# Output projection over three and a half row chunks, with one head group spread into spare columns and half-row pairs

## The chip, the core and the metric

The kernel runs on one core of a Trainium2 chip. The metric is the device time of one launch in microseconds (us). Five engines work side by side, each through its own queue of instructions: TensorE (PE in the profile) multiplies matrices into the eight PSUM banks, VectorE (DVE), ScalarE (ACT) and GpSimd (POOL) do the elementwise work, and SyncE (SP) issues most of the DMAs.

## The reference

What is computed, cut to its parts (B = 1, S = 2048, D = 448, 16 heads of 28, four segments of 512, F = 1792, all in bf16):

```python
g = sigmoid((x * gate_w).sum(-1))                      # one gate per row of x
# a: attention with a memory, over N = 4 segments of L = 512
q, k, v = heads(x @ wq), heads(x @ wk), heads(x @ wv)
for s in range(4):
    p = softmax(qs @ ks.T * 28**-0.5 + causal_mask)
    a_dot = p @ vs
    a_mem = (phi(qs) @ M) / (phi(qs) @ z + 1e-6)       # phi(t) = t + 1 if t > 0 else exp(t)
    o = sigmoid(beta) * a_mem + (1 - sigmoid(beta)) * a_dot
    M += phi(ks).T @ vs ; z += phi(ks).sum(rows)
a = concat(o) @ wo
# b: a token-mixing MLP over the rows
b = (gelu(layernorm(x).T @ w1 + b1) @ w2 + b2).T
out = g * a + (1 - g) * b
```

## The kernel before

The program is written as a list of operations with their reads and writes (`op(...)`), and the order in which each engine runs them is written out in the dictionary `ORDER`, one text per engine. A word names an operation; `@4` gives the PSUM bank (or buffer) that it takes, and `u0-3*3` stands for three operations in a row. `plan` walks through these texts, gives out the banks and adds a wait wherever an operation reads or overwrites another's result. Each engine's queue is strictly in order.

The names that matter here:

- `lok`, `loq`, `lot` with `prk`, `prq`, `prx`, `prt`: the projections. The contraction over D = 448 rows is cut into three chunks of 128 rows and one of 64. Two outputs share one 128-row operation for their 64-row chunks: `lo...` runs two products of 64 rows, one on the upper and one on the lower half of the array, into two PSUM banks, and then each output's `pr...` adds its three full chunks. In `pair`, the `lo` comes first.
- `sc`, `exp`, `mask`, `pv`: scores of up to four heads side by side on four strips of 32 rows, their exponential on ScalarE into a probability buffer, the causal mask on GpSimd, and the product with the values. There is one set of four banks (0 to 3) for the scores, so that a score waits for the exponential before it. The other four banks (4 to 7) are shared by all the other products.
- Unit `u` = 4 * segment + head group. After `pv{u}`, VectorE transposes (`ta`), takes reciprocals (`rec`), scales both parts (`oa`, `om`); the sum (`o`) runs on GpSimd or VectorE into `ob[:, u % 2]`, and VectorE transposes it again (`ot`) into `oT`, which holds the queries' place in memory. In the first segment there is no memory part, and `oa` writes `ob` itself.
- `wo0` to `wo15`: the output projection of 128 rows each. A head has 28 rows but takes a strip of 32, so four head groups of four heads take four chunks of 128 rows in `oT`, with 16 idle rows in each. `wo_sb` holds the weights in the same layout, its spare rows zeroed once by a memset on VectorE (`wo0` there, `R_wo`), and filled by seven DMAs (`ldwo`). Each tile is four products of 128 rows by 448 columns. `ag` then applies the gate in ScalarE or VectorE.
- `u{ft}-{k}` (first MLP matrix, 14 x 16 products) and `y{T}-{ft}` (second, 16 x 14 products), `fin{T}` (VectorE, joins both parts) and `out{T}` (SP, store). Their weights stream through a ring of three slots (`ldw1`, `ldw2`), each loaded in four pieces.
- `gq`, `gk`: DMAs that gather the last head group of queries and keys from spare columns of the other three. `tk`: DMA transposes of the keys. `dtx`: those of x.

TensorE instructions come in layouts: full (128 rows by 128 columns), column-split (four of 128 by 32, used in stretches that also hold a `pv` or `mst`), pairs of 64 rows (`lo`), strips of 32 rows (`sc`), and 32 by 32 (`mem`).

Of the kernel before, what the change touches and what calls it, by code (L numbers as in the profile page):

```python
# [5 lines left out]
ACT = mybir.ActivationFunctionType  # L6
# [38 lines left out]

# [29 lines left out]
class Sched:  # L75
# [13 lines left out]
    def op(self, eng, fn, reads=(), writes=(), name=None, dma=False, out=False, cost=100.0, prio=0.0, mode="f",  # L89
           nbytes=0, rel=0.0, port=False, take=None, use=(), alt=None, space=None,  # L90
           hold=HOLD):
# [42 lines left out]
        for r in reads:  # L134
            if r.last_write is not None:
                need(r.last_write)
            if r.psum and eng != "PE":
                for rd in r.reads:
                    if rd.eng != "PE" and (rd.eng != o.eng or o.eng is None):
                        need(rd)  # L140
        for r in writes:
            w = r.last_write
# [8 lines left out]
        for r in writes:  # L151
            r.last_write = o
            r.reads = []
        self.ops.append(o)
        return o

    def plan(self, order):
# [17 lines left out]

        def ready(o, banks):
            users = [held.get((g.pool, int(b))) for g, b in zip(o.take, banks)]
            return all(d.idx in done for d in o.deps + o.order) and all(g is None or g.left == 0 for g in users)

        while any(queue.values()):  # L180
            n = len(line)
            for e in ENGINES:
                while queue[e] and ready(*queue[e][0]):
                    o, banks = queue[e].pop(0)
                    assert len(banks) == len(o.take)
                    for g, b in zip(o.take, banks):
# [102 lines left out]
btr@7 lok0_0 lok0_2 prk0_0 prx0_3 prk0_2 prk0_1 lok1_2@45 loq1_0@67 prk1_2 prq1_0 prx1_3 prq1_1 loq1_2@46 loq0_0  # L289
loq0_2 prq0_2 prq1_2 prq0_1 prq0_2h prq1_2h prq0_0 lot4@45 lot6@67 prt7 prt6 sc0_0 prt4 prt5 lok1_0@67 prk1_0 prk1_1  # L290
sc0_1 lok2_0@45 prk2_0 prk2_1 lok2_2@67 prx2_3 prk2_2 sc0_2 u0-0@4*3 u1-0@5*5 u0-3*3 u3-0@6 u1-5 u3-1 sc0_3 u0-6
u2-0@7*3 u3-2 u0-7 u2-3 u1-6*2 u2-4 u1-8*3 sc0_4 u0-8*7 u1-11*2 u0-15 u1-13*3 u2-5*3 sc1_0 u2-8*2 u3-3*5 u2-10*5
u3-8*2 sc1_1 u3-10 u5-0@4*3 u4-0@5 u2-15 u4-1 u3-11*3 u4-2 u3-14*2 u4-3 sc1_2 u4-4*3 u5-3 u4-7*3 pv1@7 u4-10*3
u5-4*4 u4-13*3 u6-0@6*3 sc1_3 u6-3 u5-8*2 pv0@7 u6-4 u5-10*5 sc1_4 u7-0@5*4 u6-5*4 u5-15 u6-9 mst0@7 sc2_0 u6-10*3
u7-4*2 u6-13*3 u8-0@4*2 u7-6*2 u8-2*3 u7-8 sc2_1 u7-9*2 pv2@6 u8-5 u7-11*3 u8-6 u7-14*2 sc2_2 loq2_0@67 prq2_0
u8-7*5 prq2_1 u8-12*4 mem1 loq2_2@57 prq2_2 prq2_2h u9-0@6*10 u10-0@5*2 u9-10*2 u11-0@7 sc2_3 u9-12*4 pv3@4 u11-1*7
sc2_4 u10-2*5 u11-8*2 pv4@4 u11-10 u12-0@6 sc3_0 u11-11*3 u10-7*2 u11-14*2 u10-9*2 u13-0@4*5 sc3_1 u10-11*3 u12-1
u10-14 pv5@7 u10-15 u13-5*4 u12-2*3 sc3_2 lot8@57 u12-5 prt9 u12-6 u13-9*4 sc3_3 u12-7*3 u13-13*2 u12-10*2 u13-15
u12-12*4 prt8 sc3_4 wo0#1@7 lok3_0@45 prk3_1 prk3_0 pv6@7 sc4_0 lot10@65 prt11 mst1@4 prt10 wo1@7 sc4_1 loq3_0@45
pv7@6 prq3_1 prq3_0 lok3_2@67 sc4_2 prk3_2 prx3_3 wo3@5 wo2@6 mem2 y1-0@4*6 y0-0@6*8 y1-6*3 sc4_3 loq3_2@57 prq3_2  # L300
prq3_2h y1-9*2 y0-8 y1-11*3 sc4_4 y0-9*5 y3-0@7 pv8@4 y2-0@5*2 sc5_0 y3-1 y2-2*2 y3-2*2 y2-4 y3-4*4 sc5_1 y2-5*4
wo5@4 y3-8*2 sc5_2 pv9@6 y3-10*3 wo4@4 y3-13 sc5_3 y2-9*3 y5-0@6 y2-12*2 wo6@7 sc5_4 y5-1*4 wo7@4 pv10@5 sc6_0
y5-5*8 pv11@4 sc6_1 mst2@5 y5-13 y6-0@7*7 sc6_2 lot12@45 prt12 y6-7*2 prt13 y6-9*2 mem3 lot14@64 prt14 prt15 y6-11*3
y4-0@6*3 sc6_3 y4-3*11 sc6_4 wo9@4 y7-0@5*2 wo8@6 sc7_0 pv12@7 y7-2*2 wo11@4 y7-4*2 sc7_1 y9-0@7*2 pv13@4 y7-6*4
y8-0@6 sc7_2 y8-1 y7-10*4 y8-2*2 y9-2*2 y8-4 y9-4 sc7_3 y9-5*3 wo10@4 pv14@5 y8-5 sc7_4 y8-6*3 y9-8 y11-0@5 y8-9*3
y9-9*3 y8-12*2 y11-1*7 pv15@4 y10-0@6 y11-8*5 y9-12*2 y10-1*5 y11-13 y10-6*8 wo15@4 wo13@5 wo14@6 y14-0@7*4
y15-0@4*3 y14-4 y15-3*2 y13-0@5 y14-5 y15-5 y13-1*2 y14-6 y13-3*2 y14-7*5 wo12@6 y13-5*4 y15-6 y13-9 y12-0@6*2
y13-10 y14-12*2 y12-2*3 y13-11*2 y12-5 y13-13 y12-6*8 y15-7*7 y15-0#1@5 y15-1#1 y15-2#1 y15-3#1 y15-4#1 y15-5#1
y15-6#1 y15-7#1 y15-8#1 y15-9#1 y15-10#1 y15-11#1 y15-12#1 y15-13#1""",
    "ACT": """  # L310
ldwv0 ldgw ldwv1 ldwv2 ldwvb ldwkb ldb1 ldb2 cpv2 cpv0 gt0 gt2 cpv1 gt3 gt1 ek0_0 cpk0_1 cpk0_3 cpk1_2 cpq1_0 cpq0_3
cpk1_3 ek0_1 cpq1_3 cpq1_2 cpq0_2 cpq1_1 cpq1_2#1 cpq0_2#1 cpq0_0 eq1_2 cpv7 cpv6 gt7 tb gt6 exp0_0@2 cpv5 gt4 gt5
cpk1_1 exp0_1@3 cpk2_1 cpk2_0 cpk2_3 cpk2_2 exp0_2@4 cpq2_3 ek0_2 exp0_3@0 eq1_1 eq1_0 exp0_4@1 gsq0 gsq1 gvh0
exp1_0@5 ek1_0 gth0 gth1 exp1_1@6 gsq2 eq1_3 gsq3 ek0_3 gvh3 gth2 exp1_2@0 gsq4 gth3 exp1_3@1 ek1_2 gth4 exp1_4@2
gsq5 ek1_1 exp2_0@3 gsq6 gth5 gvh6 exp2_1@4 gth6 gsq7 ek1_3 exp2_2@5 gth7 ek2_0 cpq2_0 gsq8 cpq2_2 eq2_1 cpq2_2#1
eq2_2 eq2_0 gvh8 exp2_3@6 gsq9 ek2_1 exp2_4@0 gth9 gth8 exp3_0@1 gsq11 gvh11 exp3_1@2 gsq10 gvh10 gth11 exp3_2@3
gth10 exp3_3@4 gsq13 gt9 gsq12 cpv8 gt8 exp3_4@0 cpk3_1 gth12 eq2_3 exp4_0@5 gt11 cpv10 gt10 ag1 exp4_1@6 gth13
cpq3_1 exp4_2@1 cpq3_0 ag2 eq3_0 cpk3_3 ag3 ek2_3 eq3_1 ek2_2 exp4_3@2 exp4_4@7 exp5_0@0 eq3_2 exp5_1@3 exp5_2@4
exp5_3@5 exp5_4@6 ag7 exp6_0@1 ag6 exp6_1@2 eq3_3 exp6_2@7 cpv12 gt12 cpv14 gt14 cpv15 gt15 cpv13 gt13 exp6_3@0
exp6_4@3 exp7_0@4 ag8 exp7_1@5 exp7_2@6 exp7_3@1 exp7_4@2 ag10 ag15 ag13""",  # L320
# [39 lines left out]
def build_kernel(nc, X, WQ, WK, WV, WO, BETA, W1, B1, W2, B2, GW, OUT):  # L360
# [796 lines left out]
    for u in range(16):  # L1157
# [5 lines left out]
        if u >= 4:  # L1163
            wo_tile(u - 4)
# [60 lines left out]
```

## Time and profile before

| | |
|---|---|
| time, median of 3 runs | 171.65 us (171.44 to 171.79) |
| the profiled execution's own time | 171.96 us |
| its span, first to last instruction | 170.2 us |
| TensorE busy | 166.1 us (98%), 2319 products |
| VectorE busy | 140.1 us (82%) |
| ScalarE busy | 130.7 us (77%) |
| GpSimd busy | 58.8 us (35%) |
| granted TensorE clock | 1.00 |
| moved by DMA | 25.16 MB, mean 148 GB/s |

The span is what the profile's times refer to; the launch takes 1.76 us beside it. Busy time is the union of an engine's instructions. In rows of groups and of the timeline stand the engine, the line of the kernel, the operation, output and input, and the count; a row of the timeline begins with its start and its length in us. Products overlap each other in the array, so that the length of one (some 350 ns for 448 columns) is longer than the step from one start to the next.

### The profile page before, as it was taken

The numbers are of one execution on the slowest core, as the hardware profiler recorded it, in microseconds if no ns is written. First come the engines' busy times: TensorE is split into PE (matmuls) and PEld (weight loads), VectorE is DVE, ScalarE is ACT, GpSimd is POOL, SyncE is SP. The second block draws the span as 40 slices with busy tenths as digits, with TensorE's granted clock in tenths as the row PEclk, the third lists the DMA queues.
The fourth block names the chain that finished last, engine by engine and source line by source line (L and its number), as shares of the span: only waits on it lengthen the run. The fifth ranks groups of instructions, "written<-read, shape, count | busy, mean of one in ns | idle before, by whom it ended". The sixth has DMA issues, their size and how long they took to land.

```text
span 170.2 us, 5519 instructions
## 1 busy us (share of the span) xinstructions
PE 166.1 (98%) x2319; PEld 79.8 (47%) x2323; DVE 140.1 (82%) x325; ACT 130.7 (77%) x163; POOL 58.8 (35%) x93
## 2 busy tenths in 40 slices
PE   8999999999999999999999999999999999999994
PEld 2334433444545545544445444444544444555553
DVE  3088989959798999999999999999888697897133
ACT  0359999999999999899999988888997798603000
POOL 5000236440261018133256164347518318500000
PEclk9999999999999999999999999999999999999999
DMA  6998999784799544493049602577700252755103
GB/s 141 224 264 291 251 238 215 218 181 143 181 209 277 114 131 95 135 212 79 15 127 224 158 0 62 147 156 208 213 0 6 64 154 73 212 178 169 35 4 108
DMA packets 52631, 25.16 MB, mean 148 GB/s; under 512 B 17134, under 2 KB 52366, under 8 KB 52606
## 3 DMA queue, kind: packets, MB, share of 16 engines
q1 hardware_dynamic: 51814, 24.22, 58.7%
q10 hardware_dynamic: 792, 0.58, 1.8%
q8 instruction: 18, 0.29, 0.7%
q14 instruction: 7, 0.06, 0.1%
HBM read 18.76 MB, written 2.36 MB: 124 GB/s over the span
## 4 chain that ended last, share of the span: by engine, by line
PE 94%; DMA 3%; ACTq 1%; issue 1%; POOL 0%; DVE 0%; POOLq 0%
PE t L264 79%; PE t L941 8%; PE t L971 5%; DMA t<-in_A_wv_dram 3%; PE t L824 1%; PE t L1017 1%; ACTq L505 1%; ACTq L526 0%; DVE t L1095 0%; POOL t L524 0%; POOL t L591 0%; POOL t L567 0%; POOL t L590 0%; POOL t L584 0%; POOLq L1210 0%
## 5 line engine op out<-in xcount | busy, mean ns | idle before, releaser
L264 PE MATMUL t<-t 128*32 128x448 bf16 (+9 forms) x1554 | 141.6, 351 | 1.0 <-issue 0.6
L264 PEld LDWEIGHTS t<-t 128*32 128x32 bf16 (+2 forms) x1558 | 65.0, 97 | 63.2 <-issue 13.6
L950 ACT ACTIVATE t<-t 128x2048 bf16<-128x2048 f32 x40 | 75.1, 1877 | 6.9 <-PE t L941 6.3
L953 POOL TENSOR_SCALAR_AFFINE_SELECT t<-t 128x512 bf16<-128x512 bf16 x64 | 42.6, 680 | 52.7 <-ACT t L950 51.5
L941 PE MATMUL t<-t 28*128 28x512 bf16 (+3 forms) x256 | 15.8, 301 | 0.0
L999 POOL TENSOR_TENSOR t<-t 128x448 bf16<-128x448 f32 x8 | 9.8, 1220 | 16.4 <-DVE t L995 8.4
L1095 DVE SCALAR_TENSOR_TENSOR t<-t 128x448 bf16<-128x448 f32 (+2 forms) x17 | 10.8, 645 | 4.9 <-PE t L264 4.8
L985 DVE STREAM_TRANSPOSE t<-t 128x512 f32<-128x512 f32 x16 | 11.4, 711 | 2.6 <-PE t L971 2.3
L1049 ACT ACTIVATE t<-t 128x448 bf16<-128x448 f32 x9 | 6.5, 722 | 7.4 <-PE t L264 7.3
L971 PE MATMUL t<-t 128*32 128x512 bf16 (+3 forms) x256 | 11.5, 300 | 0.0
L893 POOL TENSOR_TENSOR t<-t 128x4 f32<-128x4 f32 x4 | 4.3, 1068 | 20.3 <-DVE t L906 16.7
L1006 DVE STREAM_TRANSPOSE t<-t 128x512 bf16<-128x512 bf16 x16 | 11.1, 693 | 0.1
L941 PEld LDWEIGHTS t<-t 28*128 28x128 bf16 x256 | 4.5, 92 | 14.0 <-ACT t L950 7.1
L884 DVE BATCH_NORM_STATS2 t<-t 128x6 f32<-128x448 bf16 x16 | 9.3, 612 | 0.6 <-DMA t<-in_A_x_dram 0.6
L786 ACT ACTIVATE t<-t 128x448 bf16<-128x448 f32 x12 | 6.4, 544 | 4.1 <-PE t L264 4.0
L1053 DVE TENSOR_SCALAR t<-t 128x448 bf16<-128x448 f32 x7 | 5.2, 740 | 5.1 <-PE t L264 5.0
L971 PEld LDWEIGHTS t<-t 128*32 128x32 bf16 x256 | 6.5, 97 | 5.6 <-issue 1.0
L1067 ACT ACTIVATE t<-t 128x448 f32<-128x448 f32 x14 | 8.8, 640 | 0.1
L1080 DVE SCALAR_TENSOR_TENSOR t<-t 128x448 bf16<-128x448 f32 x14 | 8.5, 622 | 0.4 <-ACT t L1078 0.4
L995 DVE SCALAR_TENSOR_TENSOR t<-t 128x448 f32<-128x448 f32 x12 | 8.8, 731 | 0.1
L747 ACT ACTIVATE t<-t 128x512 bf16<-128x512 bf16 x12 | 7.6, 635 | 1.4 <-DVE t L704 1.4
L1075 DVE SCALAR_TENSOR_TENSOR t<-t 128x448 f32<-128x448 f32 x14 | 8.5, 615 | 0.1
(75 smaller groups left out, 136.9 us busy)
## 6 DMA issues: line engine op xcount, KB each, us to landing
t<-in_B_w_dram SPq DMA_DIRECT2D x52, 256.0 KB, 3.9
t<-in_A_x_dram SPq DMA_DIRECT2D x4, 448.0 KB, 4.9
out_dram<-t SPq DMA_DIRECT2D x15, 112.0 KB, 2.1
t<-in_B_w_dram SPq DMA_DIRECT2D x8, 128.0 KB, 2.5
t<-in_A_wv_dram ACTq DMA_DIRECT2D x4, 112.0 KB, 4.4
t<-in_A_wq_dram SPq DMA_DIRECT2D x1, 336.0 KB, 5.2
spare_heads<-t SPq DMA_DIRECT2D x8, 32.0 KB
spare_heads<-t SPq DMA_DIRECT2D x16, 16.0 KB
```

The source lines that it names most:

```text
L264: last = e.matmul(out[q], w[:, q], x, skip_group_check=True, **kw)
L884: op("DVE", lambda e: e.bn_stats(st6[:, t, :], xh[:, t, :]), reads=[R_x[t]], writes=[R_st6[t]], name=f"bns{t}", cost=512, prio=P_PROJ - 10 ...
L941: last = e.matmul(bank(hl)[:, c0 : c0 + w], kT[r, hg, s * 512 + j * 128 : s * 512 + j * 128 + 128], qT[r, hg, s * 512 + 128 * j : s * 512 ...
L950: op("ACT", lambda e: e.activation(pslot(g), ps[:, 0:4, :], ACT.Exp, scale=SCALE), reads=R_bank[0:4], writes=[g.res], take=g, name=f"exp{p ...
L953: op("POOL", lambda e, c0=c0: e.affine_select(pslot(g)[:, :, c0 : c0 + 128], pslot(g)[:, :, c0 : c0 + 128], pattern=[[0, 4], [1, 128]], co ...
L971: last = e.matmul(bank(cb)[32 * ((hl + hg) % 4) : 32 * ((hl + hg) % 4) + 32, 128 * j : 512], vaug[:, 4 * s + j, 32 * h : 32 * h + 32], psl ...
L985: dv(lambda e: e.transpose(tt[:, ia, :], bank(cb)[:, 0:512]), [bres(cb)], [R_tt[ia]], "ta", 630, use=(cb,))
L995: dv(lambda e: e.scalar_tensor_tensor(n3[0], n3[0], oc, rb[0], op0=ALU.mult, op1=ALU.mult), [R_tt[ia], R_rec[tb], R_omcol], [R_tt[ia]], "o ...
L999: op("POOL", lambda e: e.tensor_tensor(o3, n3[0], n3[1], op=ALU.add), reads=[R_tt[ia], R_tt[im]], writes=[R_ob[tb]], name=f"o{u}", cost=12 ...
L1006: dv(lambda e: e.transpose(oT[:, hg, s * 512 : s * 512 + 512], o), [R_ob[tb]], qres(hg, s), "ot", 635)
L1067: op("ACT", lambda e: e.activation(gg[:, q, :], bank(b)[:, 0:D], ACT.Square, bias=b1s[:, ft : ft + 1], scale=math.sqrt(GC)), **buse(b), re ...
L1095: op("DVE", lambda e: e.scalar_tensor_tensor(outst[:, p, c0:c1], bank(b)[:, 0 : c1 - c0], omg[:, T : T + 1], ag(T)[:, c0:c1], op0=ALU.mult ...
```

## The change

The output projection's contraction is repacked. Head groups 1 to 3 keep their strips, and the first 12 of the 28 rows of each head of group 0 go into the spare columns of `ob` for groups 1 to 3 (four rows into each of the three strips with the same index); so they become part of the three full chunks. The other 16 rows of each of these four heads make a half chunk of 64 rows. It is written to every second column of `ob[:, 0]`, transposed with it, and copied by two DMAs for each segment (`go`) into `olo`, so that one half of the partitions holds it for the first tile of each pair and the other half for the second. `wo_sb` is loaded to match: `ldwo` (six), `ldws` (four, the spare rows), `ldwl` (eight, the half chunk twice), and its memset is dropped.

```diff
+    def wo_pair(T0):
+        s = T0 // 4
+        bs, sums = [Bank(), Bank()], [Sum(4), Sum(4)]
+        half = T0 % 4 // 2 * 128
+        def lo(e):
+            for k in range(2):
+                r = slice(64 * k, 64 * k + 64)
+                last = mm(e, bank(bs[k])[:, 0:D], olo[r, s, half : half + 128], wo_sb[r, 0, :], **sums[k].flags())
+            return last
+        op("PE", lo, reads=R_olo[2 * s : 2 * s + 2] + [R_wo[8]], writes=[bres(b) for b in bs], take=bs, name=f"lw{T0}",
+           mode="h", cost=pe_cost(448) + 4, prio=P_WO + T0, adds=True)
+        for T, b, sm in zip((T0, T0 + 1), bs, sums):
...
-            for hg in range(NHG):
+                for hg in range(1, NHG):
-                last = mm(e, bank(b)[:, 0:D], oT[:, hg, T * 128 : T * 128 + 128], wo_sb[:, hg, :], cols,
-                          start=(hg == 0), stop=(hg == NHG - 1))
+                    last = mm(e, bank(b)[:, 0:D], oT[:, hg, T * 128 : T * 128 + 128], wo_sb[:, hg, :], cols, **sm.flags())
```

In `pv_unit`, group 0 writes its result in two parts, `ox` (into the spare columns) and `oy`; in the first segment these are copies of the scaled part, later the additions:

```diff
-        o = ob[:, tb, :]
+        o = ob[:, hg, :]
+        if hg:
+            outs = [("", ocols[:, :, 0:DH], lambda x: x, [R_ob[hg]], 1.0)]
+        else:
+            spread = ob[:, 1:NHG, :].rearrange("p g (b c) -> p g b c", c=32)[:, :, :, DH:32]
+            outs = [("x", spread, lambda x: x[:, :, 0:12].rearrange("p b (g i) -> p g b i", g=3), [R_obx], 0.5),
+                    ("y", o.rearrange("p (b c z) -> p b c z", c=16, z=2)[:, :, :, 0], lambda x: x[:, :, 12:DH], [R_ob[0]], 0.6)]
...
-        dv(lambda e: e.transpose(oT[:, hg, s * 512 : s * 512 + 512], o), [R_ob[tb]], qres(hg, s), "ot", 635)
+        dv(lambda e: e.transpose(oT[:, hg, s * 512 : s * 512 + 512], o), [R_ob[hg]] + ([R_obx] if hg else []), qres(hg, s), "ot", 635)
+        if hg == 0:
+            src = oT[:, 0, s * 512 : s * 512 + 512].rearrange("p (a k t) -> p k a t", a=2, k=2)
+            for k in range(2):
+                op("SP", lambda e, k=k: e.dma_start(olo[64 * k : 64 * k + 64, s, :].rearrange("p (a t) -> p a t", a=2),
+                                                    src[0:128:2, k]),
+                   reads=qres(0, s), writes=[R_olo[2 * s + k]], name=f"go{s}_{k}", dma=True, cost=600, nbytes=32768)
```

The weights, the memsets and the pairs:

```diff
-    op("DVE", lambda e: e.memset(ob[:], 0.0), writes=R_ob, name="ob0", cost=500, prio=P_PROJ)
+    op("DVE", lambda e: e.memset(ob[:, 0, :], 0.0), writes=[R_ob[0]], name="ob0", cost=300, prio=P_PROJ)
-    op("DVE", lambda e: e.memset(wo_sb[:].bitcast(U32), 0), writes=R_wo, name="wo0", cost=896 / 0.96 + 10, prio=P_PROJ)
...
+            load(f"ldws{q}", wo_sb[32 * q + DH : 32 * q + 32, 1:NHG, :],
+                 heads[q, 0:12, :].rearrange("(g i) m -> i g m", i=4), 4 + q, 12)
+        for k in range(2):
+            for q in range(4):
+                load(f"ldwl{k}{q}", wo_sb[64 * k + 16 * q : 64 * k + 16 * q + 16, 0, :], heads[q, 12:DH, :], 8, 16)
...
+        free = "first" not in A and isinstance(bs[0], Bank)
+        sums = [Sum(4) for _ in bs]
...
-           cost=pe_cost(max(A["n"], B["n"])) + 4, prio=prio, hold=wait)
+           cost=pe_cost(max(A["n"], B["n"])) + 4, prio=prio, hold=wait, adds=free)
```

With `adds`, the operations that add into one bank no longer depend on each other: whichever comes first opens the sum, and whichever comes last closes it (`Sum.flags`). So a `lo` or `lw` may stand behind one or all of its `pr` or `wo`. In `mm2` the column split also applies to the last 128 columns of tile 15.

All five texts of `ORDER` are new. Of TensorE's, from the projections, the third and fourth parts of them and the end:

```diff
-btr@7 lok0_0 lok0_2 prk0_0 prx0_3 prk0_2 prk0_1 lok1_2@45 loq1_0@67 prk1_2 prq1_0 prx1_3 prq1_1 loq1_2@46 loq0_0
-loq0_2 prq0_2 prq1_2 prq0_1 prq0_2h prq1_2h prq0_0 lot4@45 lot6@67 prt7 prt6 sc0_0 prt4 prt5 lok1_0@67 prk1_0 prk1_1
+btr@7 lok0_0 lok0_2 prk0_0 prx0_3 prk0_2 prk0_1 prt7@4 prx1_3@5 prk1_2@6 lot6@7 lok1_2 loq0_0 loq0_2 prq0_2 prq0_0
+prt6 prq1_2@4 prq0_2h prq1_1@5 prq1_2h@6 loq1_0@7 loq1_2 prq0_1 prq1_0 prk1_1@4 sc0_0 lok1_0@5 lot4@67 prk1_0 prt5
...
+u7-1 u6-8*4 u7-2*2 u6-12 u7-4*3 u6-13*3 sc2_0 u7-7*7 pv2@4 u7-14*2 sc2_1 mst0@6 u8-0@4*2 prq2_1@5 prq2_0@7 loq2_0
+sc2_2 u8-2*4 prq2_2@5 u8-6*4 prq2_2h@6 loq2_2 mem1 u8-10*2 u9-0@5 u8-12 u9-1*8 u8-13*2 u11-0@6 sc2_3 u9-9*3 pv3@7
...
+lot10@57 u12-6*3 prt11 u12-9*7 prt10 sc3_4 mst1@7 prk3_1@4 pv6@6 prk3_0@7 lok3_0 sc4_0 prq3_1@5 prq3_0@7 wo0@6
+loq3_0 lw0@4 sc4_1 wo1 pv7@5 prk3_2@6 wo3@7 lok3_2@4 lw2@5 sc4_2 wo2 prx3_3 y0-0@6*5 mem2 y0-5*9 prq3_2h@4 prq3_2@5
...
+y8-12*2 y9-4 sc7_4 lw10 y9-5*5 pv14@5 y10-0@6*7 y9-10*2 pv15@5 y11-0@7 y10-7 y11-1*3 y10-8*2 y9-12*2 y11-4*5
+y10-10*2 y11-9*3 y10-12 y11-12*2 lw14@45 y10-13 wo14 wo15 wo12@7 y12-0@6*2 lw12@5 wo13 y13-0@4*4 y15-0@7 y13-4*2
```

On VectorE the end reads `ta15 rec15 om15 oa15 b2g3 fin9 ot14 ot15 fin11`, with `o14` and `o15` at the end of GpSimd's text; before, it was `om15 oa15 o15 ot15` on VectorE.

More of the change, by code (lines that the diff above doesn't have):

```diff
@@ L44, with __init__, flags @@
                  "free", "hold", "tile", "cols")
+class Sum:
+    def __init__(self, n):
+        self.n = self.left = n
+    def flags(self):
+        self.left -= 1
+        return {"start": self.left == self.n - 1, "stop": self.left == 0}
 class Bank:
@@ L134, in op @@
         for r in reads:
-            if r.last_write is not None:
-                need(r.last_write)
+            for w in r.adds or [r.last_write]:
+                if w is not None:
+                    need(w)
             if r.psum and eng != "PE":
@@ L174, in plan, with untaken @@
         line, done = [], set()
+        def untaken(o):
+            return [g for g in o.take if g.bank is None]
         def ready(o, banks):
-            users = [held.get((g.pool, int(b))) for g, b in zip(o.take, banks)]
+            users = [held.get((g.pool, int(b))) for g, b in zip(untaken(o), banks)]
             return all(d.idx in done for d in o.deps + o.order) and all(g is None or g.left == 0 for g in users)
@@ L184, in plan @@
                     o, banks = queue[e].pop(0)
-                    assert len(banks) == len(o.take)
-                    for g, b in zip(o.take, banks):
+                    assert len(banks) == len(untaken(o))
+                    for g, b in zip(untaken(o), banks):
                         g.bank = int(b)
@@ L298 @@
[L298 to L307, printed above, removed]
@@ new lines @@
+ag10 ta14 rec14 om14 oa14 ta15 rec15 om15 oa15 b2g3 fin9 ot14 ot15 fin11 fin10 fin13 fin12 fin14 fin15 fin15#1""",
+    "POOL": """
+szb szg mhalf oo0 og0 id0 oo1 v0 v1 og1 id1 rstd0 rstd4 og2 mask0_0_0 rstd8 mask0_1_1 mask0_1_3 rstd12 oo2 mask0_4_1
+mask0_4_3 mask0_3_0 mask0_2_2 mask1_1_1 mask0_2_2#1 mask1_1_3 mask1_2_2 mask1_2_2#1 mask1_0_0 oy0 ox0 mask2_0_0
+mask1_3_0 mask1_4_1 mask1_4_3 mask2_2_2 mask2_2_2#1 mask2_1_1 mask2_1_3 mask2_3_0 mask2_4_1 mask2_4_3 mask3_0_0
+mask3_1_1 mask3_1_3 oy4 ox4 mask3_2_2 mask3_2_2#1 o5 mask3_3_0 mask3_4_1 mask3_4_3 o6 o7 mask4_2_2 mask4_2_2#1
@@ L668, in lo @@
         def lo(e):
-            for P, b, cs, c, rows in parts:
-                last = mm(e, bank(b)[:, 0 : P["n"]], P["w"](c, rows), P["x"](c, rows), start="first" not in P, stop=False)
+            for (P, b, cs, c, rows), sm in zip(parts, sums):
+                last = mm(e, bank(b)[:, 0 : P["n"]], P["w"](c, rows), P["x"](c, rows),
+                          **(sm.flags() if free else {"start": "first" not in P, "stop": False}))
             return last
@@ L998, in pv_unit, with add @@
                "om", 535, port=True)
-            op("POOL", lambda e: e.tensor_tensor(o3, n3[0], n3[1], op=ALU.add), reads=[R_tt[ia], R_tt[im]],
-               writes=[R_ob[tb]], name=f"o{u}", cost=1280, port=True, prio=pr,
-               alt=("DVE", lambda e: e.tensor_tensor(o3, n3[0], n3[1], op=ALU.add), 535))
+            for nm, dst, part, res, f in outs:
+                def add(e, dst=dst, part=part):
+                    return e.tensor_tensor(dst, part(n3[0]), part(n3[1]), op=ALU.add)
+                op("POOL", add, reads=[R_tt[ia], R_tt[im]], writes=res, name=f"o{nm}{u}", cost=1280 * f, port=True, prio=pr,
+                   alt=("DVE", add, 535 * f))
@@ L1091, in mm2 @@
             op("PE", lambda e, cols=False, ft=ft: mm(e, bank(b)[:, 0 : c1 - c0], w2c[:, ft, t2_ * 128 : t2_ * 128 + 128],
-                                                     uT[:, ft, c0:c1], cols and not c0, start=(ft == 0), stop=(ft == NFT - 1)),
+                                                     uT[:, ft, c0:c1], cols, start=(ft == 0), stop=(ft == NFT - 1)),
                reads=[R_slot[r][ft // 4]] + (R_uT if ft == 0 else [R_uT[ft]]), writes=[bres(b)] + ([] if ft else [R_wo_y[T]]),
@@ L1162, in build_kernel @@
         pv_unit(u)
-        if u >= 4:
-            wo_tile(u - 4)
-    for T in range(12, 16):
-        wo_tile(T)
+        if u >= 4 and u % 2:
+            wo_pair(u - 5)
+    for T in (12, 14):
+        wo_pair(T)
     for i, (f_, a) in enumerate(mlp):
```

183 lines of the change are left out of this document (99 added, 84 removed).

## The prediction

> **What bounds the kernel now.** I read the page first (busy shares, clock, chain of waits), then the waits of TensorE alone, then its groups with shapes kept apart, then its timeline.
>
> ```profile
> span 170.2 us, 5519 instructions
> PE 166.1 (98%) x2319; PEld 79.8 (47%) x2323; DVE 140.1 (82%) x325; ACT 130.7 (77%) x163; POOL 58.8 (35%) x93
> PEclk9999999999999999999999999999999999999999
> PE 94%; DMA 3%; ACTq 1%; issue 1%; POOL 0%; DVE 0%; POOLq 0%
> ...
> PE t L622 <- PEq L1210: 0.8, 1, 0.8
> PE t L264 <- issue: 0.6, 4, 0.2
> PE t L264 <- DMA t<-in_A_wv_dram: 0.3, 1, 0.3
> ```
>
> The clock is full in every slice, and the chain that ends last is TensorE for 94% of the span. The last three rows are the whole list of TensorE's waits: 0.8 us before the warm-up, 0.3 us for the value weights, and four gaps of under 0.2 us. The second row has 2319 products for 2323 weight loads, so I take those four gaps for four products without a record, not for idle time. The chain shows where that unbroken work begins and ends.
>
> ```profile
> 2.94 4.78 DMA t<-in_A_wv_dram
> 7.71 0.14 issue
> ...
> 149.95 17.94 PE t L264 x390
> 167.88 0.03 issue
> 167.91 0.35 DVE t L1095
> ```
>
> So from 7.85 us to 167.9 us the time is a sum of matrix products; before it stands a load, behind it one last DVE operation and its store, and the change touches neither. What is taken from TensorE's queue comes off the end, unless a new wait takes its place. That is why I price TensorE by the start-to-start time, not by the mean of one instruction (353 ns), which overlaps its neighbours.
>
> **Prices on TensorE.** The timeline gives whole stretches between two groups of scores (L941).
>
> ```profile
> 28.28 2.82 PE L264 MATMUL t<-t 128*128 128x448 bf16 x14
> 31.04 0.40 PE L941 MATMUL t<-t 28*128 28x512 bf16 x4
> 31.36 2.63 PE L264 MATMUL t<-t 128*128 128x448 bf16 x13
> 33.93 0.40 PE L941 MATMUL t<-t 28*128 28x384 bf16 x8
> ...
> 99.23 3.39 PE L264 MATMUL t<-t 128*128 128x448 bf16 x17
> 102.55 0.40 PE L941 MATMUL t<-t 28*128 28x512 bf16 x4
> ```
>
> Start to start, 14 products take 2.76 us, 13 take 2.57 and 17 take 3.32. The differences give 0.19 us for one product of 448 columns ((3.32 - 2.57) / 4 = 0.1875, 2.76 - 2.57 = 0.19; I use 0.189), and what is left over is 0.10 to 0.12 us: the change from the full array to the four row strips of the scores. Back from scores costs as much: four 512-column scores side by side take 0.32 us to the next start, of which 512 columns are 0.189 x 512/448 = 0.216. So a switch of the array's layout costs about 0.105 us. The column-split form (128*32, four at a time) costs the same 0.189 per four: the final 17.94 us row is 80 groups of 448 columns, 14 of 320 and 14 single products of 128, by columns 15.1 + 1.9 + 0.8 = 17.8.
>
> The change needs one more price: two products of 64 rows that run beside each other.
>
> ```profile
> 24.50 3.52 PE L264 MATMUL t<-t 64*128 64x512 bf16 x16
> 27.95 0.40 PE L941 MATMUL t<-t 28*128 28x256 bf16 x8
> L264 PE MATMUL t<-t 64*128 64x512 bf16 x24 | 4.3, 384 | 0.0
> ```
>
> By the code, the 16 of this stretch are two pairs (lok2_0, lok2_2) and 12 full products. 14 slots of 0.216 are 3.02; four switches (pair to full, full to pair, back, then to scores) are 0.42; together 3.44 against 3.45 read. If the halves of a pair ran in turn, it would be 3.88. A pair of halves costs one slot.
>
> **The change, part by part.** (1) Each of the 16 output tiles (wo0 to wo15) runs three full products instead of four: 16 x 0.189 = 3.02 us removed. (2) Eight lw operations add one pair slot each: 8 x 0.189 = 1.51 us. Net -1.51.
>
> (3) Switches. I split both written TensorE orders into runs of one layout (full and column-split count as one, pairs, scores, memory products). Before: 52 full runs, 40 of scores, 3 memory, 18 of pairs: 113 runs, 112 switches. After: 50, 40, 3 and 22: 115 runs, 114 switches. The eight lw stand in runs of their own only where no neighbour was at hand; the freed order inside a pair lets the old lo stand next to scores (loq2_0 sc2_2, lok3_0 sc4_0), next to each other (lot6 lok1_2 loq0_0 loq0_2), or next to an lw (loq3_0 lw0). Two more switches: 2 x 0.105 = +0.21. The bounds: lone runs for all eight would be +16 switches, +1.68; no new one, 0.
>
> The Trainium skill, TensorEngine Tiling (Array Packing), section Tiling Modes, Key Properties, says that changing the tiling mode drains the engine. The stretches above agree and price it at 0.10 to 0.12 us; by that rule with lone pairs the change would give -1.51 + 1.68 = +0.17.
>
> (4) The last store's column split (y15#1) is spelled differently, but in the new order lw12 cuts the final run off from pv15, so it runs whole as before: 0.
>
> (5) VectorE loses the wo0 memset and part of ob0, and keeps one whole addition and one partial (o13, oy8) of four; the result of head group 0 is written in two parts (ox, oy), mostly on GpSimd.
>
> ```profile
> L586 DVE MEMSET t<- 128x896 uint32 x1 | 0.8, 805 | 1.0 <-PEq L1210 1.0
> L1001 DVE TENSOR_TENSOR t<-t 128x448 bf16<-128x448 f32 x4 | 2.5, 621 | 0.1
> L999 POOL TENSOR_TENSOR t<-t 128x448 bf16<-128x448 f32 x8 | 9.8, 1220 | 16.4 <-DVE t L995 8.4 <-DVE t L997 4.8 <-DVE t L910 3.2
> ```
>
> The memset lies before 2 us, under the 7.85 us wait for the weights: 0. GpSimd gets eight whole additions as before and seven partial ones; at no more than 1.22 each that is under 8.6 us more on an engine that is 35% busy: 0 as load. New waits: ot of groups 1 to 3 waits for ox of group 0, which stands one to three units earlier, with the state sums and gelu steps of VectorE behind it; and in the first segment oy0 and ox0 stand on GpSimd ahead of the masks of the third score pair, for which pv waits. GpSimd is idle for 65% of the span and each part is under 1.22, so I take 0 for both; uncovered they would cost one such part, 1.2. As latency it matters once, at the last unit: o15 moves from VectorE to GpSimd and stands before ot15, for which wo14 waits.
>
> ```profile
> 150.02 0.71 DVE L985 STREAM_TRANSPOSE t<-t 128x512 f32<-128x512 f32 x1
> ...
> 152.41 0.62 DVE L1001 TENSOR_TENSOR t<-t 128x448 bf16<-128x448 f32 x1
> 153.06 0.71 DVE L1006 STREAM_TRANSPOSE t<-t 128x512 bf16<-128x512 bf16 x1
> ```
>
> Before, ot15 ends at 153.77, and the 22 products behind pv15 last until 149.95 + 22 x 0.189 = 154.11: 0.34 us of cover. After, the chain is 1.22 - 0.62 = 0.60 us longer plus two hops between engines, estimated at 0.1 together; TensorE has the same 22, then lw14 with two switches (0.40) and y10-13 (0.19), 0.59 more. The cover shrinks to about 0.2. I take 0, with 0 to 0.4 as bounds (the upper end if VectorE also stands behind fin9 and ot14, which are queued between).
>
> (6) DMA. SP issues 19 more transfers: six instead of seven for the head-group rows of WO, four for the spare rows, eight for the half-row copies, and eight go copies of the transposed group 0. SP is close to full early.
>
> ```profile
> 44.74 1.68 SPq L555 DMA_DIRECT2D t<-in_B_w_dram  x3
> 46.46 1.19 SPq L754 DMA_TRANSPOSE t<-t  x1
> 47.70 2.13 SPq L555 DMA_DIRECT2D t<-in_B_w_dram  x2
> 49.87 0.93 SPq L576 DMA_DIRECT2D t<-in_A_wo_dram  x2
> t<-in_B_w_dram SPq DMA_DIRECT2D x52, 256.0 KB, 3.9
> 51.41 2.01 PE t L264 x40
> ```
>
> An issue takes 0.4 to 0.6 us (0.93 for the two of WO). The load with least room that I found is ldw1_3_2, the third of the first row: issued at about 45.9, landing 3.9 later at 49.8, and used by u6-8 in the stretch 51.41 to 53.42: at least 1.6 us of room. In the new order 51 issues stand ahead of it, as before (five for WO instead of one, fewer of the others, one transpose less), so it does not move: 0. The go copies are due long before their lw: go3 stands behind out7, near 143 us, and lw14 comes near 152 us. What waits behind a go on SP is the next W2 block, whose ring slot TensorE has mostly not yet left.
>
> (7) Scores against exponentials. From 105 to 146 us the exponentials set the pace.
>
> ```profile
> 110.31 1.88 ACT L950 ACTIVATE t<-t 128x2048 bf16<-128x2048 f32 x1
> 112.70 1.88 ACT L950 ACTIVATE t<-t 128x2048 bf16<-128x2048 f32 x1 [0.51 <-PE t L941]
> 115.19 1.88 ACT L950 ACTIVATE t<-t 128x2048 bf16<-128x2048 f32 x1 [0.62 <-PE t L941]
> 117.57 1.88 ACT L950 ACTIVATE t<-t 128x2048 bf16<-128x2048 f32 x1 [0.50 <-PE t L941]
> ```
>
> The shortest step is 1.88 + 0.50 = 2.38 us. A stretch of ten products with one 512-score group is 10 x 0.189 + 0.216 + 0.21 = 2.32, so it waits 0.06. Pricing both orders like this, I count five such stretches before and six after: +0.06, within the error, taken as 0.
>
> Sum: -3.02 + 1.51 + 0.21 = -1.30 us. The profiled execution took 171.96 us, 1.76 outside its span, and would take 170.66; the median of the three runs is 0.31 lower, and I predict 171.65 - 1.30 = 170.35, written 170.4.
>
> **The rivals.** A, the sum goes through, with waits inside the bounds: -0.3 if the score waits of today go too (about 0.3 us in all), +0.5 for new ones (0.4 at wo14, 0.06 of scores): 170.0 to 170.9.
>
> B, a new wait eats part of it: each lw holds two of the four free PSUM banks from its first product to the second eviction, where a tile held one.
>
> ```profile
> L1049 ACT ACTIVATE t<-t 128x448 bf16<-128x448 f32 x9 | 6.5, 722 | 7.4 <-PE t L264 7.3
> ```
>
> At lw12 the bank is wo15's: wo12, two y products and a switch cover 5 x 0.189 + 0.105 = 1.05 us against an eviction of 0.72 plus hops. If all eight pairs waited 0.1, it would be 171.2. Against it: the lo pairs hold two banks already, and the waits above name no eviction. The Trainium skill, on the same page, section Restrictions and Gotchas, warns of just this PSUM pressure under row tiling; no run so far shows it.
>
> C, slower: a W1 block comes late because of the added issues. The new issues before 60 us are nine or so, 9 x 0.48 = 4.3 us; if all of it reached the 1.6 us of room at u6-8 (or a like block), TensorE would idle 2.7 us: 173.0. It decides from 1.6 + 1.3 = 2.9 us of delay. Against it: the count of 51 above.
>
> D, the change doesn't do what it says: the two halves run in turn. +8 x 0.189 = 1.51: 171.9, no change. Against it: the 3.45 us stretch.
>
> **How the numbers follow.** A change of 0.2% (0.34 us) is about what a measurement of this kernel can tell. A 0.76, B 0.11, C 0.10, D 0.03. A is faster, B mostly (0.07 of it), C is slower but for a small lateness (0.02 of it within the bound), D the same. Faster 0.83, same 0.09, slower 0.08. The range holds A and most of B: 169.9 to 171.2.
>
> **What would show it.** Right: 16 products of 64 rows by 448 columns in pairs with one start, each pair in one slot; no wait of TensorE over 0.4 us; the last product near 166.6 us. Wrong: a wait of TensorE before a 64-row product, named after an eviction (B); one before u products named after in_B_w (C); 64x448 products that start 0.19 us apart (D). A time under 169.9 would mean that the layout switches cost more than read here, since the pairs moved beside scores save most of them.

## The result and the profile after

| | before | after |
|---|---|---|
| time, median of 11 runs each | 171.62 us (171.36 to 171.83) | 170.68 us (170.13 to 171.5) |
| ratio to before, 95% interval | | 0.9948 [0.9933, 0.9962] |
| the same kernels once more (17 and 6 runs) | 171.8 us | 171.11 us, 0.9957 [0.9941, 0.9974] |
| the profiled execution's own time | 171.96 us | 170.68 us |

The change makes the kernel faster by 0.89 us by the first ratio (0.65 to 1.15) and by 0.74 us by the second; forecast were 1.30. The time lies in the range. The page of the changed kernel, its list of TensorE's waits, and the ends of its chain of waits:

```profile
span 168.9 us, 4944 instructions
PE 164.7 (98%) x2022; PEld 78.5 (47%) x2026; DVE 136.7 (81%) x321; ACT 130.6 (77%) x164; POOL 64.3 (38%) x100
PE 94%; DMA 3%; ACTq 1%; issue 1%; POOL 0%; DVE 0%; POOLq 0%
...
PE t L651 <- PEq L1280: 0.8, 1, 0.8
PE t L282 <- issue: 0.6, 3, 0.3
PE t L282 <- DMA t<-in_A_wv_dram: 0.3, 1, 0.3
...
2.96 4.43 DMA t<-in_A_wv_dram
7.39 0.14 issue
7.52 1.42 PE t L282 x8
...
148.46 18.07 PE t L282 x175
166.52 0.02 issue
166.55 0.35 DVE t L1165
```

The picture is the same: TensorE is 94% of the chain, and it runs almost without a break from the first value product to its last. The stretch to compare is that one: 7.85 to 167.88 us before, 7.52 to 166.52 after, 160.03 against 159.00, so -1.03 us. The two profiled executions differ by 1.28; the rest is the start, 0.33 earlier because the load of the value weights took 4.43 us here and 4.78 there, less 0.08 behind the last product. That the profiled execution came out within 0.02 of its forecast (170.66) is therefore a coincidence.

One of the three "issue" gaps is new and longer than a missing record. It shows in the timeline and on SP's queue of the changed kernel:

```profile
18.10 1.18 SPq L535 DMA_TRANSPOSE t<-in_A_x_dram  x1
...
23.51 0.40 PE L973 MATMUL t<-t 28*128 28x384 bf16 x8
24.16 0.81 PE L282 MATMUL t<-t 128*128 128x512 bf16 x3 [0.26 <-issue]
```

and of the kernel before:

```profile
18.46 1.18 SPq L515 DMA_TRANSPOSE t<-in_A_x_dram  x1
...
24.18 0.40 PE L941 MATMUL t<-t 28*128 28x384 bf16 x8
24.50 1.79 PE L264 MATMUL t<-t 64*128 64x512 bf16 x8
```

From the start of the score group (sc0_1) to the next product the step is 0.32 us before and 0.65 after: the changed kernel waits 0.32 us ahead of prk2_1. The SP row is dtx2_1, the transposed third chunk of x for that product; the last of its 16 completion steps is at 23.13 us before (4.67 after its issue) and at 24.07 after (5.97 after it), 0.09 ahead of prk2_1. Before, lok2_0 needs it at 24.50; the new order needs it at 23.84. SP issues the same transfers in the same order up to dtx2_1 in both kernels; why it takes 1.3 us longer stays open.

### The profile page after: what moved, and what is told of

It reads as the page before. It is cut to its first block, busy times and chain, and to the rows that moved or that the text cites. A ratio compares the mean times of both kernels' runs of the same rounds, so it can differ in the third digit from the quotient of the medians.

```text
span 168.9 us, 4944 instructions
## 1 busy us (share of the span) xinstructions
PE 164.7 (98%) x2022; PEld 78.5 (47%) x2026; DVE 136.7 (81%) x321; ACT 130.6 (77%) x164; POOL 64.3 (38%) x100
## 4 chain that ended last, share of the span: by engine, by line
PE 94%; DMA 3%; ACTq 1%; issue 1%; POOL 0%; DVE 0%; POOLq 0%
PE t L282 79%; PE t L973 8%; PE t L1003 5%; DMA t<-in_A_wv_dram 3%; PE t L856 1%; PE t L1076 1%; ACTq L525 1%; ACTq L546 0%; DVE t L1165 0%; POOL t L544 0%; POOL t L620 0%; POOL t L587 0%; POOL t L619 0%; POOL t L615 0%; POOLq L1280 0%
## 5 line engine op out<-in xcount | busy, mean ns | idle before, releaser
L282 PEld LDWEIGHTS t<-t 128*32 128x32 bf16 (+2 forms) x1261 | 63.7, 97 | 63.8 <-issue 15.3
L985 POOL TENSOR_SCALAR_AFFINE_SELECT t<-t 128x512 bf16<-128x512 bf16 x64 | 43.3, 688 | 43.0 <-ACT t L982 40.0
L1040 POOL TENSOR_TENSOR t<-t 128x448 bf16<-128x448 f32 (+2 forms) x13 | 13.3, 1026 | 19.0 <-DVE t L1033 14.4
L1165 DVE SCALAR_TENSOR_TENSOR t<-t 128x448 bf16<-128x448 f32 (+2 forms) x17 | 10.7, 642 | 10.6 <-PE t L282 10.5
L1119 ACT ACTIVATE t<-t 128x448 bf16<-128x448 f32 x10 | 7.1, 732 | 7.6 <-PE t L282 7.6
L1003 PE MATMUL t<-t 128*32 128x512 bf16 (+3 forms) x256 | 11.5, 300 | 0.0
L818 ACT ACTIVATE t<-t 128x448 bf16<-128x448 f32 x13 | 6.8, 546 | 4.2 <-PE t L282 4.2
L1003 PEld LDWEIGHTS t<-t 128*32 128x32 bf16 x256 | 6.7, 96 | 5.3 <-issue 0.7
L808 DVE SCALAR_TENSOR_TENSOR t<-t 128x512 bf16<-128x512 bf16 x12 | 8.5, 712 | 0.1
L1143 DVE TENSOR_SCALAR t<-t 128x448 f32<-128x448 f32 x10 | 6.5, 676 | 2.4 <-ACT t L1137 2.3
```

The costliest lines, as they stand in the source:

```text
L282: last = e.matmul(out[q], w[:, q], x, skip_group_check=True, **kw)
L985: op("POOL", lambda e, c0=c0: e.affine_select(pslot(g)[:, :, c0 : c0 + 128], pslot(g)[:, :, c0 : c0 + 128], pattern=[[0, 4], [1, 128]], co ...
L1003: last = e.matmul(bank(cb)[32 * ((hl + hg) % 4) : 32 * ((hl + hg) % 4) + 32, 128 * j : 512], vaug[:, 4 * s + j, 32 * h : 32 * h + 32], psl ...
L1040: return e.tensor_tensor(dst, part(n3[0]), part(n3[1]), op=ALU.add)
L1165: op("DVE", lambda e: e.scalar_tensor_tensor(outst[:, p, c0:c1], bank(b)[:, 0 : c1 - c0], omg[:, T : T + 1], ag(T)[:, c0:c1], op0=ALU.mult ...
```

## The experiments

Each run's stretch is read like the two above, from the first value product to the end of the last product in the chain of waits. It varies by itself: its first 14 products alone take 2.60 to 2.77 us in the ten profiled executions. Times are medians, and each ratio is to the kernel before on the same chip (171.62 us for after, 171.83 for e1 to e4, 171.8 for the others).

| run | stretch, us | time, us | ratio to before |
|---|---|---|---|
| before | 7.85 to 167.88 = 160.03 | 171.62 | 1 |
| after | 7.52 to 166.52 = 159.00 | 170.68 | 0.9948 |
| after_again | 7.99 to 166.81 = 158.82 | 171.11 | 0.9957 [0.9941, 0.9974] |
| e1_x2_first | 8.26 to 167.06 = 158.80 | 170.72 | 0.9934 [0.9912, 0.9955] |
| e2_x2_late | 8.11 to 167.28 = 159.17 | 171.64 | 0.9985 [0.9966, 1.0004] |
| e3_lone_pairs | 8.39 to 169.57 = 161.18 | 173.34 | 1.0082 [1.0058, 1.0105] |
| e4_order_only | 7.55 to 168.23 = 160.68 | 173.03 | 1.0060 [1.0040, 1.0080] |
| e5_lone_clean | 7.95 to 167.48 = 159.53 | 171.41 | 0.9978 [0.9965, 0.9992] |
| e6_pairs_adjacent | 8.12 to 166.73 = 158.61 | 170.75 | 0.9928 [0.9910, 0.9946] |
| e7_tail_split | 7.85 to 167.71 = 159.86 | 171.81, one run | |

**The chunk of x earlier and later.** On SP, dtx2_1 is issued ahead of two other loads, or behind one more block of W1:

```diff
 # e1_x2_first, SP
-ldw1_0_0 dtx2_0 ldx12 dtx2_1 ldw1_0_1
+dtx2_0 dtx2_1 ldx12 ldw1_0_0 ldw1_0_1
 # e2_x2_late, SP
-dtx2_0 ldx12 dtx2_1 ldw1_0_1
+dtx2_0 ldx12 ldw1_0_1 dtx2_1
```

> The changed kernel with one edit on SP: the transposes of the third chunk of x (dtx2_0, dtx2_1) are issued ahead of ldx12 and of the first W1 block instead of around them. Theory 1: the wait of 0.32 us that TensorE has before prk2_1 in the changed kernel ends with the landing of dtx2_1 (23.92 us, product at 24.16 us), and 0.3 us of the 1.30 forecast was lost there. Then dtx2_1 lands near 23.0 us, the wait is gone, TensorE's work from lot2 to the last product shrinks from 158.8 to 158.5 us, and the time is 170.68 - 0.3 = 170.4 us. Rival: VectorE's statistics or the first W1 block, now later, take over and the time stays at 170.7 us or rises.

> The changed kernel with dtx2_1 issued one W1 block later (behind ldw1_0_1). Theory 1: it lands about one block (0.9 us) later, the wait before prk2_1 grows from 0.3 to about 1.2 us, and the time is 170.68 + 0.9 = 171.6 us: the start of the second set of projections hangs on that DMA alone. Rival: the gap before prk2_1 has another cause (a bank, an eviction), it stays at 0.3 us and the time at 170.7 us.

The timeline of e1_x2_first, where both transposes stand in one SP row:

```profile
12.70 5.05 SPq L535 DMA_TRANSPOSE t<-in_A_x_dram  x2
...
24.27 0.40 PE L973 MATMUL t<-t 28*128 28x384 bf16 x8
24.60 1.69 PE L282 MATMUL t<-t 128*128 128x512 bf16 x7
```

and of e2_x2_late:

```profile
19.01 1.18 SPq L535 DMA_TRANSPOSE t<-in_A_x_dram  x1
...
24.13 0.40 PE L973 MATMUL t<-t 28*128 28x384 bf16 x8
24.92 1.46 PE L282 MATMUL t<-t 128*128 128x512 bf16 x6 [0.39 <-issue]
```

The step behind sc0_1 is 0.33 us with the chunk early (no wait) and 0.79 with it late (0.46 of wait). So the wait is that transfer: it lands at 19.68 us in e1_x2_first, and at 24.83 in e2_x2_late, again 0.09 ahead of the product. The size is smaller than I expected, by time as by trace: e2_x2_late loses 0.5 to 0.6 us against the changed kernel, of which the trace shows 0.17 to 0.35 in the stretch. The reason is that the wait has two ends, and both move. In e2_x2_late the landing is 0.76 later than in the changed kernel, but TensorE also starts 0.59 later (first column of the table). The changed kernel run again starts 0.47 later with a landing 0.21 later (24.28), and waits 0.15 instead of 0.32 (step 23.89 to 24.37). A late start alone is no relief: e3_lone_pairs starts latest of all, at 8.39, its transfer lands at 24.86, and it waits 0.24. e1_x2_first's gain in time, 0.2 to 0.4 us, is no more than the uncertainty of two such ratios, and its stretch is 0.02 to 0.20 shorter; that the wait goes is shown, the size of the gain is not.

> The changed kernel once more, beside the next three kernels on one chip. Theory (the time is the sum of TensorE's terms): 0.9948 of the kernel before, as in the first measurement, so 170.7 to 170.9 us; the trace again shows the wait of 0.3 us ahead of prk2_1 for the transposed chunk of x. Rival (that wait was a chance of one execution): no such wait, and the time the same.

The ratio is 0.9957, so the gain is there again. The wait is there too, with half its size, 0.15 us: so it is no chance of one execution, though its size varies.

**Six pairs moved away from their neighbours.** lw0, lw2, lw4, lw6, lw8 and lw10 stand in runs of their own; the work is the same:

```diff
 # e3_lone_pairs, PE (three of six)
-loq3_0 lw0@4 sc4_1 wo1 pv7@5
+loq3_0 sc4_1 wo1@4 lw0 pv7@5
-sc5_2 lw4@7 wo5 y2-8
+sc5_2 wo5@7 lw4 y2-8
-sc5_4 lw6@45 y5-7 pv10@7
+sc5_4 y5-7 lw6@45 pv10@7
```

> The changed kernel with six of the eight lw taken away from their neighbours, so that they stand in runs of their own: 122 changes of layout instead of 114, the same products otherwise. Theory 2: each change costs 0.107 us on the path, +0.86 us, 171.5 us, the before kernel's time. Rival: the drain is hidden behind the weight loads or the waits of the scores, and the time stays within 0.2 us of 170.7 us.

It costs 2.15 to 2.3 us against the changed kernel by the ratios, 2.18 in the stretch, more than twice the sum of its eight switches. TensorE's waits name what the sum lacks:

```profile
PE t L282 <- DVE t L1165: 0.4, 1, 0.4
PE t L973 <- ACT t L982: 0.2, 1, 0.2
PE t L282 <- DVE t L1123: 0.2, 1, 0.2
```

The first is lw6, which waits for a bank. How it comes about shows in VectorE's rows of the timeline, first of the changed kernel (the gate of tile 4, the eviction of tile 2, then lw6):

```profile
112.34 0.74 DVE L1123 TENSOR_SCALAR t<-t 128x448 bf16<-128x448 f32 x1 [0.17 <-PE t L282]
...
115.73 0.67 DVE L1165 SCALAR_TENSOR_TENSOR t<-t 128x448 bf16<-128x448 f32 x1
...
116.72 0.36 PE L282 MATMUL t<-t 64*128 64x448 bf16 x2
```

then of e3_lone_pairs:

```profile
114.66 0.74 DVE L1123 TENSOR_SCALAR t<-t 128x448 bf16<-128x448 f32 x1 [0.84 <-PE t L282]
...
118.47 0.68 DVE L1165 SCALAR_TENSOR_TENSOR t<-t 128x448 bf16<-128x448 f32 x1
...
119.20 0.36 PE L282 MATMUL t<-t 64*128 64x448 bf16 x2 [0.35 <-DVE t L1165]
```

ag4 (L1123) needs lw4, which now closes the sum of tile 4 behind wo5. VectorE stands idle 0.84 us for it, with fin2 (L1165) seven operations further back in the same queue; fin2 slips by 2.74 us where TensorE's order has slipped by 1.8, and lw6 needs its bank. Of the 2.74, 2.32 are there at ag4 already; the other 0.42 come because two operations between them (L805 and L808) take 0.48 and 1.06 us here and 0.25 and 0.69 in the changed kernel. In e5_lone_clean, where lw6 is moved and lw4 is not, they take 0.25 and 0.69, and lw6 does not wait. A pair that ends 0.7 us later on TensorE thus costs 0.35 us there five microseconds on, through a queue on which neither stands. This is the bank wait of rival B, which none of the changed kernel's pairs has. The other parts are prk3_2 0.37 late behind pv7, sc7_0 0.26 late for its exponential and pv14 0.2 late.

**Three pairs moved without that.** lw6, lw8 and lw10 move by one product; what lies between two score groups stays the same, and ag4 is left alone:

```diff
 # e5_lone_clean, PE
-sc5_4 lw6@45 y5-7 pv10@7
+sc5_4 y5-7 lw6@45 pv10@7
-y7-0@5*3 wo9@7 lw8@6 sc7_0
+y7-0@5*2 wo9@7 lw8@6 y7-2 sc7_0
-sc7_4 lw10 y9-5*5
+sc7_4 y9-5 lw10 y9-6*4
```

> Three of the eight half-row pairs (lw6, lw8, lw10) are moved by one product away from the scores or pairs beside them; what lies between two groups of scores stays the same work. Theory A (a lone pair costs its switches and nothing else): three more switches, 3 x 0.107 = +0.32 us over the changed kernel, about 171.0 us. Theory B (each lone pair costs more, because the banks that it holds or waits for come late, as when six were moved): +0.8 to +1.3 us, 171.5 to 172.0 us, with a wait ahead of lw6 or lw8.

Against the changed kernel on the same chip it loses 0.36 us by the ratios (0.9978 against 0.9957), where the sum has 0.32. In the stretch it loses 0.71: 0.32 of switches, 0.15 because this execution waited 0.30 for the chunk of x against 0.15, 0.19 ahead of pv14 and 0.04 ahead of lw8. The wait ahead of pv14 (L1003) is one for a bank, by the same way as in e3_lone_pairs: lw10 closes the sum of tile 10, ag10 (L1123) starts later, and pv14 takes its bank. In the changed kernel and then in this run:

```profile
144.59 0.74 DVE L1123 TENSOR_SCALAR t<-t 128x448 bf16<-128x448 f32 x1
...
145.48 0.73 PE L1003 MATMUL t<-t 128*32 128x512 bf16 x16
```

```profile
145.55 0.74 DVE L1123 TENSOR_SCALAR t<-t 128x448 bf16<-128x448 f32 x1 [0.43 <-PE t L282]
...
146.44 0.73 PE L1003 MATMUL t<-t 128*32 128x512 bf16 x16
```

pv14 starts 0.15 us after the end of ag10 in both. So theory A holds for the switches, which cost their sum, and the times show no more than that (the two ratios leave about 0.35 us either way). By the trace a part of theory B is there too, 0.23 us of waits, most of it not ahead of lw6 or lw8 but ahead of pv14.

**Two switches fewer.** lw12 follows lw14, and its two tiles go to banks 2 and 3, which the scores no longer need; the chunk of x comes early as in e1_x2_first:

```diff
 # e6_pairs_adjacent, PE
-lw14@45 y10-13 wo14 wo15 wo12@7 y12-0@6*2 lw12@5 wo13 y13-0@4*4
+lw14@45 lw12 y10-13 wo14 wo15 wo12 wo13 y12-0@6*2 y13-0@5*4
```

> The transposed chunks of x first on SP (as in the run e1_x2_first), and lw12 directly behind lw14, its two tiles in two banks of the scores that are free by then. Theory A (the terms add): the wait ahead of prk2_1 goes (-0.3, of which 0.1 came back as two short waits in e1_x2_first) and two switches go (2 x 0.107 = 0.21): 0.4 us under the changed kernel, 170.3 us; the cover of ot15 grows by one pair slot, so no wait ahead of wo14. Theory B (what is saved in one place is waited for in the next): as e1_x2_first or no better than the changed kernel, 170.7 us, with a wait ahead of wo14 or y12.

The weight loads of the timeline, in the changed kernel and then in this one:

```profile
152.55 0.10 PEld L282 LDWEIGHTS t<-t 64*128 64x128 bf16 x2 [0.37 <-issue]
...
155.22 0.10 PEld L282 LDWEIGHTS t<-t 64*128 64x128 bf16 x2 [0.37 <-ACT t L1119]
```

```profile
21.95 0.10 PEld L282 LDWEIGHTS t<-t 64*128 64x128 bf16 x2 [0.30 <-DVE t L794]
...
152.96 0.11 PEld L282 LDWEIGHTS t<-t 64*128 64x128 bf16 x4 [0.37 <-issue]
```

One group of four loads where there were two groups of two, and no wait ahead of wo14 or y12. By the ratios it is 0.50 us under the changed kernel on the same chip (170.75 against 171.11), the fastest version here; the two intervals just overlap. The stretch shows 0.21 less than after_again, which had only 0.15 of the wait to lose: -0.15, -0.21, and +0.18 for a new wait ahead of lot4, whose bank VectorE had not copied out (the first row of the second fence). So theory A holds for the switches. Whether the wait ahead of lot4 belongs to the early chunk stays open: e1_x2_first has the same order on SP and not this wait.

**The new order without the packing.** The output projection runs four full products again, with the memset and the whole additions of before; the `lw` and their DMAs are gone, all else stays in the new order (106 switches instead of 114):

```diff
 # e4_order_only, PE (parts)
-loq3_0 lw0@4 sc4_1 wo1 pv7@5
+loq3_0 sc4_1 wo1@4 pv7@5
-lw14@45 y10-13 wo14 wo15 wo12@7 y12-0@6*2 lw12@5 wo13
+y10-13 wo14@4 wo15@5 wo12@7 y12-0@6*2 wo13@5
```

> The packing undone, the rest kept: four full chunks for each tile, group 0 in its own strips, the seven loads of WO and the memset as before; the freed order inside a pair and the new orders of all engines stay, without the lw, ox, oy, go, ldws and ldwl. 106 changes of layout instead of 114 (112 before). Theory 3: the packing alone is worth 1.51 us less 8 x 0.107 for its own changes of layout, so this kernel takes 170.68 + 0.65 = 171.3 us, between the two. Rival: the packing's 1.51 us is the whole change and the order is worth nothing: 172.2 us; or the order does it all: 170.7 us.

It is slower than the kernel before, and 1.8 to 1.9 us slower than the changed one; the stretch has +1.68 where products and switches alone give +1.51 - 8 x 0.107 = +0.65. Its timeline:

```profile
59.55 0.93 PE L282 MATMUL t<-t 128*32 128x512 bf16 x9 [0.19 <-issue]
...
152.93 1.38 DVE L1026 STREAM_TRANSPOSE t<-t 128x512 bf16<-128x512 bf16 x2
...
154.36 2.83 PE L282 MATMUL t<-t 128*32 128x448 bf16 x56 [0.27 <-DVE t L1026]
```

wo14 starts 0.44 us late, right behind ot15 (the second of the two transposes, ending 154.31). In the changed kernel ot15 ends 5.21 us after the start of pv15 and TensorE has pv15, 23 products and lw14 with its two switches (0.40) to run, 5.3 us; here the 0.40 is missing. Three `pv` come late by 0.12 to 0.19 (0.4 together against after), the wait for the chunk of x is absent (-0.3; it lands at 23.42 us), and inside prq2_0 there is a stall of 0.55 us for which the profile names nothing; it stays unexplained. So the order alone is no gain in this form: it counts on slots that the packing puts in, as behind pv15. What the order is worth beside that is not shown, since the stall is a third of the 1.68. The reverse, the packing in the old order, wasn't tried.

**The last split.** The kernel before with one edit:

```diff
-                                                     uT[:, ft, c0:c1], cols and not c0, start=(ft == 0), stop=(ft == NFT - 1)),
+                                                     uT[:, ft, c0:c1], cols, start=(ft == 0), stop=(ft == NFT - 1)),
```

> The kernel before with one edit: the last 14 products (the second part of the last output tile, 128 columns) are column-split like those ahead of them, as the changed kernel has them. Theory A (going from column-split to full products inside a run is a switch like the others): the 0.106 us ahead of the first of them goes, and nothing else changes: 171.7 us where the kernel before has 171.8. Theory B (that gap belongs to the new PSUM bank, not to the form): the gap stays.

The two last evictions, of before (with the weight loads of the full form) and then of this run:

```profile
166.91 0.78 PEld L264 LDWEIGHTS t<-t 128*128 128x128 bf16 x14 [0.27 <-DVE t L1095]
167.04 0.55 DVE L1095 SCALAR_TENSOR_TENSOR t<-t 128x320 bf16<-128x320 f32 x1 [0.27 <-PE t L264]
167.91 0.35 DVE L1095 SCALAR_TENSOR_TENSOR t<-t 128x128 bf16<-128x128 f32 x1 [0.32 <-PE t L264]
```

```profile
166.96 0.55 DVE L1095 SCALAR_TENSOR_TENSOR t<-t 128x320 bf16<-128x320 f32 x1 [0.27 <-PE t L264]
167.74 0.35 DVE L1095 SCALAR_TENSOR_TENSOR t<-t 128x128 bf16<-128x128 f32 x1 [0.23 <-PE t L264]
```

They are 0.87 us apart before and 0.78 here, and from product to product the gap of 0.106 ahead of y15-0#1 is gone. Theory A holds, at the one place where these kernels have such a change: full products inside a column-split run cost a switch. The changed kernel is free of it in another way than the expectation says: behind lw12 both parts of its last tile run in the full form. One run's time (171.81) can't show a tenth of a microsecond.

## Why the prediction was right, point by point

The sign, the mechanism and the range were right; no wait of TensorE behind its start is over 0.4 us, and its last product ends at 166.52 us (the forecast had it near 166.6; the start, 0.33 earlier, helped it there by chance). The sum was too large, by 0.3 us in the stretch and 0.4 to 0.6 by the ratios, and its terms stand as follows (a trace's step is from start to start).

```profile
L282 PE MATMUL t<-t 64*128 64x448 bf16 x16 | 2.9, 357 | 0.0
...
133.79 0.36 PE L282 MATMUL t<-t 64*128 64x448 bf16 x2
134.08 0.10 PEld L973 LDWEIGHTS t<-t 28*128 28x128 bf16 x4 [0.20 <-ACT t L982]
...
151.56 1.38 DVE L1059 STREAM_TRANSPOSE t<-t 128x512 bf16<-128x512 bf16 x2
```

- Parts 1 and 2, products (-1.51): as forecast. The sixteen half-row products are there, in eight pairs; the pair lw8 at 133.79 is followed by scores at 134.08, 0.29 = one slot of 0.189 and one switch. Rival D, 0.189 more for each pair, is excluded.
- Part 3, switches (+0.21): as forecast. The steps at changes of layout in the changed kernel, where nothing is waited for, give 0.093 to 0.125 us, most of them 0.095 to 0.112, and moving the count by +3 (e5_lone_clean) and -2 (e6_pairs_adjacent) moved the time by what 0.107 gives, within the uncertainty.
- Part 4, the last split (0): wrong. I counted the full and the column-split form as one layout. Before, their change cost 0.106 us; the changed kernel doesn't pay it: -0.10. The Trainium skill, TensorEngine Tiling (Array Packing), Tiling Modes, says without a price that a change of tiling mode drains the engine; e7_tail_split agrees, for this pair of forms too.
- Part 5, the chain to wo14 (0): right, with less to spare than thought. ot15 (the second of the two transposes in the fence's last row) ends at 152.94 and wo14 starts at 153.05: 0.11 us of cover, not 0.2. The upper end of its bounds (0.4) is about what e4_order_only pays without lw14, 0.44.
- Part 6, DMA (0): the step that failed. I looked for a late block of W1 (rival C) and found room enough, and there is no wait for in_B_w. But I didn't put the other early loads against their new users. The new order pulls the first product on the third chunk of x from 24.50 to 23.84 us, and the transfer, issued 0.36 earlier, takes 1.3 longer: +0.15 to +0.32.
- Part 7, scores against exponentials (0, estimate +0.06): seven waits of 0.04 to 0.07 instead of six, +0.05.

The terms give -1.51 + 0.21 - 0.10 + 0.32 + 0.05 = -1.03, the stretch's -1.03. That they meet to the hundredth is luck: the stretch varies by a tenth or two from one execution to the next, and the 0.05 that pv14 waits is left out. Measured are -0.74 and -0.89 with about 0.25 either way. Whether the last 0.1 to 0.3 is chance or belongs to the launch's start, which the stretch leaves out, these runs can't tell.

Rival B's mechanism is real and next to nothing in the changed kernel: its eight pairs wait for no bank, and only pv14 waits 0.05 us for the bank of tile 10. e3_lone_pairs shows it, one product further on. The Trainium skill, same page, Restrictions and Gotchas, warns of PSUM pressure under row tiling; that run agrees, and its 0.35 us came through VectorE's queue.

## What to carry to other kernels

When TensorE is the whole chain, its time is a sum of slots and layout switches, and both can be read to a hundredth or two from start-to-start steps; count every change of form as a switch, full to column-split too. When an order changes, hold each early load against its new first user, not only those that the change adds; a transfer that landed 1.4 us ahead of its use was late after the reorder. A packed pair is cheap beside scores or another pair, and moving it by one product can cost more than its switches, through an eviction queued behind it on another engine.

## What was not expected of the hardware

A change between full and column-split products inside one run costs 0.106 us (at the one place that e7_tail_split tries), as much as a change to the score strips. The same load of the value weights, issued in the same place, took 4.43 to 5.31 us in ten profiled executions, which moves the start of TensorE's work by 0.9 us, as much as the whole gain. The landing of a later load on SP, dtx2_1, moves as well, from 24.07 to 24.86 us in the four executions with one order on SP (after, after_again, e3_lone_pairs, e5_lone_clean), so that the wait for it is 0.32, 0.15, 0.24 and 0.30.
